# The first 18 microseconds of a state-space scan with a gated feed-forward: C's rows, the sums and half of g in another order

## The chip, the cores and the metric

The kernel runs on one core of a Trainium2 chip. A core has five engines that take their instructions in order, each from its own queue: TensorE (PE, with its weight loads shown as PEld), VectorE (DVE), ScalarE (ACT), GpSimd (POOL) and SyncE (SP), which here only issues DMAs. They meet at semaphores. The metric is the device time of one execution in microseconds; a run's figure is given with the median of several. All times below are of the profiled execution, counted from its start, unless said otherwise.

## The reference

Inputs are x (4 sequences, 8 heads, 768 steps, 32 channels), a (a decay for each step), B and C (16 state components). Weights are w_in (256 x 2048) and w_out (2048 x 256), which arrive in 8-byte floats.

```python
# per sequence and head, in chunks of 32 steps
cum = np.cumsum(log(clip(a, 1e-6, 1)))
L = exp(cum[i] - cum[j]) * (i >= j)
y_intra = ((C @ B.T) * L) @ x
y_inter = (C @ state) * exp(cum)
y = y_intra + y_inter
state = exp(sum(la)) * state + sum_j B[j] x[j] * exp(cum[-1] - cum[j])
# then, with the heads' channels side by side (256), for 3072 rows
h = y @ w_in
out = (h * cos(h)) @ w_out
```

## The kernel before

The 768 steps are cut into six chunks of 128. Chunk 0, with which this document deals, is cut again into two units of 64 steps (k = 0 and 1) of all four sequences, so that the feed-forward can begin early. For a unit the kernel makes, in this order of need:

- **lam**, the decays between all pairs of steps: `share_a` spreads a's rows on DVE and POOL, `spread_a` (L372) multiplies them by a 0/1 matrix on PE into a bank called a_ps, `decays0` (L380) scans the bank on DVE. Unit 0 is spread in four products of 256 columns, (k, p, i) = (0,0,0) to (0,1,1), unit 1 in (1,0,0), (1,0,1) and the whole of (1,1), which is two records of 512 columns. A float32 product shows as two records on PE.
- **the turned C and B**: C's first 128 rows of each sequence come as four DMAs (`load_c`, L113) in groups of four rows. A copy into `c0` puts them in order of row (columns 0 to 2 of four on POOL at L358, column 3 on ACT at L918). `turn_c` (L403) transposes c0 by four products and gives back `take(k)`, two scaled copies on ACT into `cuts[k]`, and `of`, a plain copy. `turn_b` (L418) transposes B's rows of a unit and copies them on ACT.
- **g**, the products of C and B (`inner(k, t)`, L461, t = 0 and 1 for the heads' halves, 16 small products each); **m**, g weighted by lam (`weights(k, q)`, L472, DVE); **sc**, B weighted by lam's last column (`weigh0`, L391, POOL).
- **y** and the new state (`finish0(k)`, L514): for unit 1 first the old state's part (L527, 32 products), then `sums` (L480, called in finish0: sc with x, 32 products, the state's sum), then m with x (L537, 64 products). y is copied on ACT to `yT`, the sums to `state0` by `take`. For unit 1 the old state's part needs `rT`, C weighted by the reach (`reach0`, L424, a product and a DVE scan, and `weigh_c`, L433, with a plain copy of C on ACT and a product on POOL).

The feed-forward goes in steps n. Step n of chunk 0 takes unit n % 2 and 256 columns of w_in: `first(n)` (L662) makes hp in two halves e, four records each half, and can run a function between the halves; `wind_k`, `wind_w`, `gate` and `gated` make hp * cos(hp) on ACT and DVE; `second(n)` (L797) adds its product with w_out to the output. A piece of weights is fetched as pairs of 32-bit words (`fetch`, L226) and turned to float32 by `grade` (L244: ACT, POOL, ACT) and `join` (L266: two DVE operations and an addition on POOL, L283).

Three things set the order of the work. Each engine runs its instructions in the order of the text below L909, which is written out by hand. SP's queue is the order of the fetches and loads at L285 to L302: a, B of unit 0, w_in 0, x of unit 0, B of unit 1, w_in 1, x of unit 1, w_out 0 and on; ACT's queue holds the four loads of C. And PSUM's banks are lent out by turns: `pair` (L72) gives two banks at a time out of two such pairs (to the first two spread products, to each half of g, to y of unit 0 once and to y of unit 1 twice), `bank` with the tags "h" and "o" gives single banks out of two each. A product into a buffer that was lent before waits until the last reader of the earlier content is done.

From L1060 on `first_steps` runs steps 0 to 3 with unit 1's y between the halves of step 0:

```python
        for q in range(2):
            weights(1, q)
        states_of = []
        first(0, lambda: states_of.extend(finish0(1)))
```

Of the kernel before, what the change touches and what calls it, by code (L numbers as in the profile page):

```python
# [8 lines left out]
FP32 = mybir.dt.float32  # L9
# [16 lines left out]
def kernel(  # L26
# [236 lines left out]
        if later:  # L263
            return rest

    def join(which, i, between=None):  # L266


        parts = held.pop((which, i), ())
        for e, (high, bits, last) in enumerate(parts):  # L270
            V.tensor_scalar(out=bits, in0=bits, scalar1=3, scalar2=0x3FFFFFFF,
                            op0=ALU.logical_shift_left, op1=ALU.bitwise_and)
            if between:
                between()
            V.scalar_tensor_tensor(out=bits, in0=high, scalar=0xC0000000, in1=bits,
                                   op0=ALU.bitwise_and, op1=ALU.bitwise_or)
            dst = kept(which, i)
            if len(parts) > 1:
                dst = dst[:, :, e * P:(e + 1) * P]
            else:  # L280
                bits, last = (ap.rearrange("p (k f) -> p k f", k=dst.shape[1])
                              for ap in (bits, last))
            G.tensor_tensor(out=dst.bitcast(U32), in0=bits, in1=last, op=ALU.add)  # L283

    for b in range(NB):  # L285
        load_c(b, nc.scalar)
    for s in range(2):
        load_b(0, s)
    fetch("in", 0)
# [1 line left out]
        load_x(0, s)  # L291
    for s in range(2):
        load_b(1, s)
    fetch("in", 1)
    for s in range(2):
        load_x(1, s)
    fetch("out", 0)
    nc.sync.dma_start(
        out=a_in, in_=a.rearrange("(u b) h (c p) -> (b h c) u p", u=NU, p=P))
# [47 lines left out]
    whose_of(1)  # L347
    G.memset(along1[:, :, 0:1], 0.0)
    G.tensor_scalar(out=a0[:, 1], in0=a0[:, 1], **clip)
    for p in range(2):  # L350
        G.tensor_tensor(out=along1[:, 2 * p:2 * p + 2, 1:], in0=a0[:, 1:2].to_broadcast([P, 2, W]),
                        in1=those[:, p::2].unsqueeze(2).to_broadcast([P, 2, W]), op=ALU.mult)
    own = ms[2][:, 3 * NB * (W + 1):3 * NB * (W + 1) + P]
    G.tensor_copy(out=own.rearrange("p (h n) -> p h n", h=H),
                  in_=mine.unsqueeze(2).to_broadcast([P, H, N]))
    c0 = loads.tile([P, 2, 2, 4, 2, N], FP32, tag="blocks", name="c0").rearrange(
        "p a b c d n -> p (a b c d n)").rearrange("p (r h n) -> p r h n", r=4, h=H)
    G.tensor_copy(out=c0[:, 0:3].rearrange("p r h n -> p h r n"), in_=c4[:, :, 0:3])  # L358
    G.memset(lead, 0.0)
    G.memset(lead[:, :, 0:1], 1.0)  # L360
    slot = const.tile([P, 2], FP32, name="slot")
# [68 lines left out]
            out=reach1.rearrange(flat), data0=ps.rearrange(flat),  # L430
            data1=lead.rearrange(flat), initial=0.0, op0=ALU.mult, op1=ALU.add)

    def weigh_c(k, of):  # L433
        c = scan.tile([P, NB, W], FP32, tag="rT", name="c1")
        of(k, c)
        rTs[k] = t = scan.tile([P, NB, W], FP32, tag="rT", name="rT")
        G.tensor_tensor(out=t, in0=c, in1=reach1[:, :, 1:], op=ALU.mult)

# [72 lines left out]
                                       scalar=reach[k // 2, s][:, p, i:i + 1],  # L511
                                       in1=after[k][:, s, p], op0=ALU.mult, op1=ALU.add)

    def finish0(k):  # L514

        m, xk = m_of[k], xrs[k]
        y = [pair("y") for _ in range(2)] if k else [pair("y")]
        at_ = [[(y[t][:, s, p * W:(p + 1) * W] if k else
                 y[0][:, s, t * P + p * W:t * P + (p + 1) * W]) for p in range(2)]
               for t in range(2) for s in range(2)]  # L520
        if k:
            old = states0.pop(k)
            for p in range(2):
                for s in range(2):
                    for q in range(4):
                        r, c0 = slice(32 * q, 32 * q + 32), W * (q % 2)
                        PE.matmul(at_[2 * (q // 2) + s][p][c0:c0 + W], lhsT=old[r, s, p],  # L527
                                  rhs=rTs[k][r, 2 * p + s], start=(p == 0), stop=False,
                                  tile_position=(32 * q, c0), skip_group_check=True)
        sums(k, [y[0][:, s, 3 * P:] for s in range(2)], lambda q, s: slice(32 * q, 32 * q + 32),  # L530
             start=(k == 0))
        for p in range(2):
            for t in range(2):
                for s in range(2):
                    ss = slice(s * W, (s + 1) * W)
                    for q in range(4):
                        PE.matmul(at_[2 * t + s][p][32 * q:32 * q + 32],  # L537
                                  lhsT=xk[ss, p, 4 * t + q], rhs=m[ss, p, 4 * t + q],
                                  start=False, stop=True,
                                  tile_position=(s * W, 32 * q), skip_group_check=True)  # L540
        if k % 2 == 0:
            yT[k // 2] = two.tile([P, 2, 2, 2 * P], FP32, tag="yT", name="yT")
        t_ = yT[k // 2][:, k % 2]
        if k:
            for t in range(2):
                ACT.copy(out=t_[:, t].rearrange("p (s i) -> p s i", s=2), in_=y[t][:, :, 0:P])
        else:
            ACT.copy(out=t_.rearrange("p t (s i) -> p s t i", s=2),
                     in_=y[0][:, :, 0:2 * P].rearrange("p s (t i) -> p s t i", t=2))
        states0[k + 1] = new = states.tile([P, 2, 2, 2 * D], FP32, tag="state0", bufs=2,  # L550
                                           name="state0")

        def take():
            for t in range(2):
                ts = slice(t * D, (t + 1) * D)
                ACT.activation(new[:, :, :, ts], y[0][:, :, 3 * P:].rearrange(
                    "p s (q d) -> p s q d", q=2)[:, :, :, ts], AF.Copy, scale=slot[:, t:t + 1])

        def add():
            dec = scan.tile([P, 2, 2, 2 * D], FP32, tag="whole", bufs=1, name="whole")  # L560
            r4 = reachs[k].rearrange("p (q s) i -> p s q i", s=2)
            for s in range(2):
                G.tensor_tensor(out=dec[:, s], in0=old[:, s],
                                in1=r4[:, s, :, W:].to_broadcast([P, 2, 2 * D]), op=ALU.mult)
            if k < 3:
                G.tensor_tensor(out=new, in0=new, in1=dec, op=ALU.add)
                return
            whole = states.tile([P, 2, 2, 2 * D], FP32, tag="state1", bufs=1, name="state1")
            for s, to_ in ((1, new), (0, whole)):
                G.tensor_tensor(out=to_[:, s], in0=new[:, s], in1=dec[:, s], op=ALU.add)  # L570
            after[3] = whole

            def exchange():
                for qs, rs in turns_of[1]:
                    nc.sync.dma_start(out=whole[rs, 1], in_=new[32 * qs.start:32 * qs.stop, 1])
            return exchange
        return take, add

    def reaches(c, b):

# [333 lines left out]
    for p, i in ((0, 0), (0, 1), (1, 0)):  # L914
        decays0(0, p, i, 2)
    tp_b = bank([P, 4, P], "tp", "o")
    turn_b(0, tp_b)()
    ACT.copy(out=c0[:, 3:4].rearrange("p r h n -> p h r n"), in_=c4[:, :, 3:4])  # L918
    spread_a(0, 1, 1, 2, "h")
    decays0(0, 1, 1, 2)  # L920
    take_c, of_c = turn_c()
    spread_a(1, 0, 0, 2, "h")
    take_c(0)
    decays0(1, 0, 0, 2)
    weigh0(0)
    grade("in", 0)
    for t in range(2):
        inner(0, t)
    spread_a(1, 0, 1, 2, "h")
    spread_a(1, 1, tag="h")  # L930
    for q in range(2):
        weights(0, q)
    take_c(1)
    join("in", 0)
    decays0(1, 0, 1, 2)
    decays0(1, 1)
    take_s0, _ = finish0(0)
    take_b = turn_b(1, tp_b)
    scan_reach = reach0(1)
    scan_reach()  # L940
    take_b()
    take_s0()
    for t in range(2):
        inner(1, t)
    weigh0(1)
    weigh_c(1, of_c)

    la = const.tile([RB, NU, P], FP32, name="la")
    cut = const.tile([RB, NU, P], FP32, name="cut")
# [110 lines left out]
    def first_steps():  # L1060

        grade("in", 1)
        for q in range(2):
            weights(1, q)
        states_of = []
        first(0, lambda: states_of.extend(finish0(1)))
        take_s1, add_s1 = states_of
        join("in", 1)
        rests = [grade("out", 0, later=True)]
        wind_k(0)  # L1070
        take_s1()
        rests.pop()()
        wind_w(0)
        first(1)
        join("out", 0)
        wind_k(1)
        gate(0)
        wind_w(1)
        gate(1)
        gated(0)  # L1080
        gated(1)
        first(2, tag=None)
        rests = [grade("in", 2, later=True)]
        wind_k(2)
        rests.pop()()
        clip_cut()
        wind_w(2)
        rests = [grade("out", 1, later=True)]
        join("in", 2)
        first(3, tag=None)  # L1090
        gate(2)
        wind_k(3)
        rests.pop()()
        rests = [grade("in", 3, later=True)]
        gated(2)
        join("out", 1)
        second(0)
        wind_w(3)
        gate(3)
        rests.pop()()  # L1100
        rests = [grade("out", 2, later=True)]
        join("in", 3)
        gated(3)
        second(1)
        clip_all()
        return add_s1, rests
# [166 lines left out]
```

## Time and profile before

| | |
|---|---|
| median of 3 runs | 364.44 us (363.73 to 365.11) |
| the profiled execution's own time | 364.44 us |
| its span from first to last instruction | 362.7 us |
| mean granted TensorE clock | 0.998 |
| PE busy, 0 to 6.2 us / 6.2 to 17.67 / 17.67 to 40 | 5.43 / 10.59 / 22.29 us |
| ACT busy in the same stretches | 1.49 / 6.09 / 18.74 us |
| DVE | 5.00 / 8.99 / 19.73 us |
| POOL | 3.91 / 5.76 / 15.98 us |
| DMA engines, mean busy share | 0.60 / 1.00 / 0.67 |

The first stretch lasts until TensorE leaves the first three spread products, the second until it begins the second half of step 0, and the third is the first part of the feed-forward. Busy time on PE counts pipelined products from start to modelled end, so it is nearly full even where the array works on small products. Idle time ahead of an instruction is put down to whatever semaphore came last. A DMA's issue and its landing are different marks: the issue is an instruction on SP or ACT, the landing is the last of 16 semaphore steps.

### The profile page before, as it was taken

The numbers are of one execution on the slowest core, as the hardware profiler recorded it, in microseconds if no ns is written. First come the engines' busy times: TensorE is split into PE (matmuls) and PEld (weight loads), VectorE is DVE, ScalarE is ACT, GpSimd is POOL, SyncE is SP. The second block draws the span as 40 slices with busy tenths as digits, with TensorE's granted clock in tenths as the row PEclk, the third lists the DMA queues.
The fourth block names the chain that finished last, engine by engine and source line by source line (L and its number), as shares of the span: only waits on it lengthen the run. The fifth ranks groups of instructions, "written<-read, shape, count | busy, mean of one in ns | idle before, by whom it ended". The sixth has DMA issues, their size and how long they took to land.

```text
span 362.7 us, 10240 instructions
## 1 busy us (share of the span) xinstructions
PE 357.0 (98%) x4070; PEld 326.0 (90%) x4070; DVE 276.0 (76%) x504; ACT 184.0 (51%) x352; POOL 239.7 (66%) x387
## 2 busy tenths in 40 slices
PE   8999999999999999999999999999999999999995
PEld 4788888889999999999989999999999999999995
DVE  7779998488876987878766877875776776688864
ACT  3597656544454346534536533545553544444552
POOL 5567767699666677674786666686666465475572
PEclk9999999999999999999999999999999999999999
DMA  7984997666583429113228202110001001001001
GB/s 138 246 284 141 189 196 122 85 125 98 134 129 58 99 51 135 14 34 76 53 53 119 23 3 75 28 33 11 0 2 31 0 3 33 0 3 29 3 17 44
DMA packets 96624, 26.43 MB, mean 73 GB/s; under 512 B 86624, under 2 KB 92480, under 8 KB 96576
## 3 DMA queue, kind: packets, MB, share of 16 engines
q1 hardware_dynamic: 95328, 25.38, 34.9%
q8 instruction: 32, 0.52, 0.6%
q10 hardware_dynamic: 1248, 0.39, 0.5%
q14 instruction: 16, 0.13, 0.1%
HBM read 22.36 MB, written 3.34 MB: 71 GB/s over the span
## 4 chain that ended last, share of the span: by engine, by line
PE 96%; DMA 2%; DVE 1%; issue 0%; ACT 0%; POOL 0%; DVEq 0%
PE o L848 35%; PE hp L672 33%; PE o L808 8%; PE m L772 7%; PE hp L772 5%; DMA bc<-in_C_dram 2%; PE y L641 2%; PE g L615 1%; PE y L489 1%; PE y L629 1%; PE g L468 1%; PE y L537 1%; PE y L527 1%; PE o L900 0%; PE tp L451 0%
## 5 line engine op out<-in xcount | busy, mean ns | idle before, releaser
L672 PE MATMUL hp<-yT,w_in 128*128 128x256 f32 x544 | 129.6, 382 | 0.1
L672 PEld LDWEIGHTS hp<-yT,w_in 128*128 128x128 f32 x544 | 99.0, 190 | 13.8 <-issue 1.4
L724 POOL TENSOR_TENSOR gd<-gT 128x256 f32<-128x256 f32 x79 | 58.1, 735 | 76.9 <-DVE gT L699 61.8
L694 ACT ACTIVATE w<-w,quarter 128x512 f32<-128x512 f32 x96 | 69.4, 723 | 65.8 <-DVE w L685 65.7
L685 DVE SCALAR_TENSOR_TENSOR w<-hp,k 128x512 f32<-128x512 f32 x96 | 65.8, 686 | 45.4 <-ACT k L679 45.2
L679 ACT ACTIVATE k<-hp 128x512 int32<-128x512 f32 x96 | 57.2, 596 | 68.6 <-PE hp L672 60.3
L699 DVE TENSOR_TENSOR gT<-hp,w 128x512 f32<-128x512 f32 x96 | 65.6, 683 | 12.2 <-ACT w L694 8.3
L848 PE MATMUL o<-words,gd 128*128 128x128 f32 x474 | 66.0, 275 | 0.0
L848 PEld LDWEIGHTS o<-words,gd 128*128 128x128 f32 x474 | 59.4, 192 | 0.0
L848 PE MATMUL o<-w_out,gT 128*128 128x128 f32 x316 | 50.4, 278 | 0.0
L848 PEld LDWEIGHTS o<-w_out,gT 128*128 128x128 f32 x316 | 45.4, 191 | 3.1
L726 POOL TENSOR_TENSOR gd<-gT,gd 128x128 f32<-128x128 f32 x79 | 39.6, 501 | 6.2
L727 POOL TENSOR_TENSOR gd<-gT,gd 128x128 f32<-128x128 f32 x79 | 39.0, 493 | 6.2
L848 PE MATMUL o<-w_out,gd 128*128 128x128 f32 x158 | 30.6, 276 | 0.0
L848 PE MATMUL o<-words,gT 128*128 128x128 f32 x158 | 30.6, 275 | 0.0
L808 PE MATMUL o<-w_out,gT 128*128 128x256 f32 x128 | 30.0, 380 | 0.0
L387 DVE TENSOR_TENSOR_SCAN lam<-arow,unit 128x512 f32<-128x512 f32 x20 | 29.9, 1496 | 0.1
L808 PEld LDWEIGHTS o<-w_out,gT 128*128 128x128 f32 x128 | 24.2, 190 | 3.6 <-POOL w_out L283 0.4
L848 PEld LDWEIGHTS o<-words,gT 128*128 128x128 f32 x158 | 24.0, 192 | 0.0
L848 PEld LDWEIGHTS o<-w_out,gd 128*128 128x128 f32 x158 | 24.0, 192 | 0.0
L772 PE MATMUL m<-m,words 128*128 128x128 f32 x168 | 23.4, 276 | 0.0
L772 PE MATMUL hp<-yT,w_in 128*128 128x128 f32 x112 | 21.7, 275 | 0.0
(130 smaller groups left out, 463.6 us busy)
## 6 DMA issues: line engine op xcount, KB each, us to landing
words<-in_moe_w_in_dram SPq DMA_DIRECT2D x8, 512.0 KB
words<-in_moe_w_out_dram SPq DMA_DIRECT2D x8, 512.0 KB
xr<-in_x_dram SPq DMA_DIRECT2D x24, 128.0 KB
arow<-a_cut SPq DMA_DIRECT2D x10, 256.0 KB
arow<-a_cut SPq DMA_DIRECT2D x10, 252.0 KB
out_dram<-sum SPq DMA_DIRECT2D x18, 128.0 KB
bc<-in_B_dram SPq DMA_DIRECT2D x24, 64.0 KB
blocks<-in_B_dram SPq DMA_DIRECT2D x16, 32.0 KB
```

The lines of the kernel that those rows point to most:

```text
L387: V.tensor_tensor_scan(out=lams[k][:, p, hs].rearrange(flat), data0=rows_.rearrange(flat), data1=unit0[:, hs].rearrange(flat), initial=0.0 ...
L672: PE.matmul(to_[:, e], lhsT=w_in[:, k, fs], rhs=y[:, k], start=(k == 0), stop=(k == KT - 1), skip_group_check=True)
L679: ACT.activation(k, hp[n], AF.Copy, bias=0.25, scale=INV_2PI)
L685: V.scalar_tensor_tensor(out=w, in0=hp[n], scalar=INV_2PI, in1=k, op0=ALU.mult, op1=ALU.subtract)
L694: ACT.activation(cos, cos, AF.Sin, bias=quarter, scale=TWO_PI)
L699: V.tensor_tensor(out=gT[n], in0=hp.pop(n), in1=cos, op=ALU.mult)
L724: G.tensor_tensor(out=d[:, 0:2], in0=g[:, 1:2].to_broadcast([P, 2, P]), in1=g[:, 3::-3], op=ALU.subtract)
L726: G.tensor_tensor(out=d[:, 2], in0=g[:, 0], in1=d[:, 0], op=ALU.subtract)
L727: G.tensor_tensor(out=d[:, 3], in0=g[:, 2], in1=d[:, 2], op=ALU.subtract)
L772: PE.matmul(dst[q], lhsT=w[q], rhs=y_[q], start=(q in (6, 1, 7)), stop=True, skip_group_check=True)
L808: PE.matmul(o[c, u][:, t], lhsT=g[:, 2 * e + t], rhs=w_out[:, 2 * j + e], start=(j == e == t == 0), stop=(j == NJ - 1 and e == 1), skip_gr ...
L848: PE.matmul(at[q], lhsT=a_[q], rhs=w[q], start=(j == 0 and q in starts), stop=(j == NJ - 1), skip_group_check=True)
```

## The change

C's fourth load goes from ACT's queue to SP's, where it stands behind a and ahead of B. On SP the loads of x of unit 1 go ahead of w_in 1. C's rows are copied in one operation on POOL, ahead of the products for `along1`; ACT's share of that copy is gone. C is transposed and its scaled copies for unit 0 are made ahead of B's transposes, and with them ahead of the spread (0,1,1). The spread (1,1) goes behind `sums` of unit 0, inside `finish0`, and for both units `sums` stands first, ahead of all of y. The copy of y of unit 0 goes behind B's copy of unit 1 on ACT. `join` of w_in 0 adds in two halves of 128 columns. The plain copy of C (`copy_c`) is made just behind `take_c(1)`, `weigh0(1)` goes ahead of the reach's scan. g of unit 1 is split: its first half stays ahead of step 0, its second half, with its weights on DVE, goes between the halves of step 0, ahead of `finish0(1)`.

```diff
@@ -263,7 +263,7 @@
         if later:
             return rest
 
-    def join(which, i, between=None):
+    def join(which, i, between=None, halves=False):
 
 
         parts = held.pop((which, i), ())
@@ -280,10 +280,15 @@
             else:
                 bits, last = (ap.rearrange("p (k f) -> p k f", k=dst.shape[1])
                               for ap in (bits, last))
+            if halves:
+                for f in (slice(0, P), slice(P, 2 * P)):
+                    G.tensor_tensor(out=dst[:, :, f].bitcast(U32), in0=bits[:, :, f],
+                                    in1=last[:, :, f], op=ALU.add)
+                return
             G.tensor_tensor(out=dst.bitcast(U32), in0=bits, in1=last, op=ALU.add)
 
-    for b in range(NB):
-        load_c(b, nc.scalar)
+    for i in range(NB):
+        load_c(i, nc.scalar if i < NB - 1 else nc.sync)
     for s in range(2):
         load_b(0, s)
     fetch("in", 0)
@@ -291,9 +296,9 @@
         load_x(0, s)
     for s in range(2):
         load_b(1, s)
-    fetch("in", 1)
     for s in range(2):
         load_x(1, s)
+    fetch("in", 1)
     fetch("out", 0)
     nc.sync.dma_start(
         out=a_in, in_=a.rearrange("(u b) h (c p) -> (b h c) u p", u=NU, p=P))
@@ -347,15 +352,15 @@
     whose_of(1)
     G.memset(along1[:, :, 0:1], 0.0)
     G.tensor_scalar(out=a0[:, 1], in0=a0[:, 1], **clip)
+    c0 = loads.tile([P, 2, 2, 4, 2, N], FP32, tag="blocks", name="c0").rearrange(
+        "p a b c d n -> p (a b c d n)").rearrange("p (r h n) -> p r h n", r=4, h=H)
+    G.tensor_copy(out=c0.rearrange("p r h n -> p h r n"), in_=c4)
     for p in range(2):
         G.tensor_tensor(out=along1[:, 2 * p:2 * p + 2, 1:], in0=a0[:, 1:2].to_broadcast([P, 2, W]),
                         in1=those[:, p::2].unsqueeze(2).to_broadcast([P, 2, W]), op=ALU.mult)
     own = ms[2][:, 3 * NB * (W + 1):3 * NB * (W + 1) + P]
     G.tensor_copy(out=own.rearrange("p (h n) -> p h n", h=H),
                   in_=mine.unsqueeze(2).to_broadcast([P, H, N]))
-    c0 = loads.tile([P, 2, 2, 4, 2, N], FP32, tag="blocks", name="c0").rearrange(
-        "p a b c d n -> p (a b c d n)").rearrange("p (r h n) -> p r h n", r=4, h=H)
-    G.tensor_copy(out=c0[:, 0:3].rearrange("p r h n -> p h r n"), in_=c4[:, :, 0:3])
     G.memset(lead, 0.0)
     G.memset(lead[:, :, 0:1], 1.0)
     slot = const.tile([P, 2], FP32, name="slot")
@@ -430,9 +435,12 @@
             out=reach1.rearrange(flat), data0=ps.rearrange(flat),
             data1=lead.rearrange(flat), initial=0.0, op0=ALU.mult, op1=ALU.add)
 
-    def weigh_c(k, of):
+    def copy_c(of):
         c = scan.tile([P, NB, W], FP32, tag="rT", name="c1")
-        of(k, c)
+        of(1, c)
+        return c
+
+    def weigh_c(k, c):
         rTs[k] = t = scan.tile([P, NB, W], FP32, tag="rT", name="rT")
         G.tensor_tensor(out=t, in0=c, in1=reach1[:, :, 1:], op=ALU.mult)
 
@@ -511,13 +519,19 @@
                                        scalar=reach[k // 2, s][:, p, i:i + 1],
                                        in1=after[k][:, s, p], op0=ALU.mult, op1=ALU.add)
 
-    def finish0(k):
+    def finish0(k, between=None):
 
         m, xk = m_of[k], xrs[k]
         y = [pair("y") for _ in range(2)] if k else [pair("y")]
         at_ = [[(y[t][:, s, p * W:(p + 1) * W] if k else
                  y[0][:, s, t * P + p * W:t * P + (p + 1) * W]) for p in range(2)]
                for t in range(2) for s in range(2)]
+        at = [y[0][:, s, 3 * P:] for s in range(2)]
+        strip = lambda q, s: slice(32 * q, 32 * q + 32)
+        if k < 2:
+            sums(k, at, strip, start=True)
+        if between:
+            between()
         if k:
             old = states0.pop(k)
             for p in range(2):
@@ -527,8 +541,8 @@
                         PE.matmul(at_[2 * (q // 2) + s][p][c0:c0 + W], lhsT=old[r, s, p],
                                   rhs=rTs[k][r, 2 * p + s], start=(p == 0), stop=False,
                                   tile_position=(32 * q, c0), skip_group_check=True)
-        sums(k, [y[0][:, s, 3 * P:] for s in range(2)], lambda q, s: slice(32 * q, 32 * q + 32),
-             start=(k == 0))
+        if k > 1:
+            sums(k, at, strip)
         for p in range(2):
             for t in range(2):
                 for s in range(2):
@@ -544,7 +558,8 @@
         if k:
             for t in range(2):
                 ACT.copy(out=t_[:, t].rearrange("p (s i) -> p s i", s=2), in_=y[t][:, :, 0:P])
-        else:
+
+        def take_y():
             ACT.copy(out=t_.rearrange("p t (s i) -> p s t i", s=2),
                      in_=y[0][:, :, 0:2 * P].rearrange("p s (t i) -> p s t i", t=2))
         states0[k + 1] = new = states.tile([P, 2, 2, 2 * D], FP32, tag="state0", bufs=2,
@@ -574,7 +589,7 @@
                 for qs, rs in turns_of[1]:
                     nc.sync.dma_start(out=whole[rs, 1], in_=new[32 * qs.start:32 * qs.stop, 1])
             return exchange
-        return take, add
+        return (take, add) if k else (take_y, take, add)
 
     def reaches(c, b):
 
@@ -914,36 +929,34 @@
     for p, i in ((0, 0), (0, 1), (1, 0)):
         decays0(0, p, i, 2)
     tp_b = bank([P, 4, P], "tp", "o")
+    take_c, of_c = turn_c()
+    take_c(0)
     turn_b(0, tp_b)()
-    ACT.copy(out=c0[:, 3:4].rearrange("p r h n -> p h r n"), in_=c4[:, :, 3:4])
     spread_a(0, 1, 1, 2, "h")
     decays0(0, 1, 1, 2)
-    take_c, of_c = turn_c()
     spread_a(1, 0, 0, 2, "h")
-    take_c(0)
     decays0(1, 0, 0, 2)
     weigh0(0)
     grade("in", 0)
     for t in range(2):
         inner(0, t)
     spread_a(1, 0, 1, 2, "h")
-    spread_a(1, 1, tag="h")
     for q in range(2):
         weights(0, q)
     take_c(1)
-    join("in", 0)
+    c1 = copy_c(of_c)
+    join("in", 0, halves=True)
     decays0(1, 0, 1, 2)
+    yT0, take_s0, _ = finish0(0, lambda: spread_a(1, 1, tag="h"))
     decays0(1, 1)
-    take_s0, _ = finish0(0)
-    take_b = turn_b(1, tp_b)
+    weigh0(1)
+    turn_b(1, tp_b)()
     scan_reach = reach0(1)
     scan_reach()
-    take_b()
+    weigh_c(1, c1)
+    yT0()
     take_s0()
-    for t in range(2):
-        inner(1, t)
-    weigh0(1)
-    weigh_c(1, of_c)
+    inner(1, 0)
 
     la = const.tile([RB, NU, P], FP32, name="la")
     cut = const.tile([RB, NU, P], FP32, name="cut")
@@ -1060,10 +1073,15 @@
     def first_steps():
 
         grade("in", 1)
-        for q in range(2):
-            weights(1, q)
+        weights(1, 0)
         states_of = []
-        first(0, lambda: states_of.extend(finish0(1)))
+
+        def unit1():
+            inner(1, 1)
+            weights(1, 1)
+            states_of.extend(finish0(1))
+
+        first(0, unit1)
         take_s1, add_s1 = states_of
         join("in", 1)
         rests = [grade("out", 0, later=True)]
```

## The prediction

> **What bounds the kernel now.** The page's line of engines comes first: TensorE (PE) is busy 98% of a span of 362.7 us. Its chain of work that ended last is PE's to 96%. So time can only be won where the chain is not PE work. The chain in order of time shows where that is (start, length, what):
>
> ```profile
> 2.99 3.89 DMA bc<-in_C_dram
> ...
> 6.93 0.52 POOL c L358
> ...
> 7.49 0.67 PE tp L407 x4
> ...
> 8.19 0.85 ACT cT L411 x2
> ...
> 9.08 0.71 PE g L468 x30
> ...
> 17.02 0.72 PE y L537 x39
> 17.74 6.24 PE hp L672 x28
> ```
>
> The fourth load of C, its copy on POOL, its turn on PE and the scaled copies on ACT lead to unit 0's products g. From 17.7 us on nearly every piece is PE's, back to back. So the whole change is worth what it moves one instruction: the first hp matmul of the second half of step 0, which starts at 17.67. I call this moment E. Everything ahead of E is filled with waits; everything behind it follows E one for one, unless a later wait takes over.
>
> The timeline of PE (start, span, instructions; in brackets idle time before and its cause) gives the order that the change alters:
>
> ```profile
> 9.08 0.73 PE L468 MATMUL g<-cT,turned 32*64 32x128 f32 x32 [0.50 <-ACT cT L411]
> 9.73 1.56 PE L376 MATMUL a_ps<-m 128*128 128x256 f32 x4
> 11.22 0.45 PE L489 MATMUL y<-xr,sc 64*32 64x64 f32 x32
> 11.49 0.90 PE L537 MATMUL y<-m,xr 64*32 64x64 f32 x64
> 12.32 0.44 PE L421 MATMUL tp<-ident,bc 128*128 128x128 f32 x2
> 12.81 0.71 PE L427 MATMUL a_ps<-m 128*128 128x260 f32 x2
> 13.45 1.09 PE L468 MATMUL g<-cT,turned 32*64 32x128 f32 x32
> 14.47 1.13 PE L672 MATMUL hp<-yT,w_in 128*128 128x256 f32 x4
> 15.53 1.11 PE L527 MATMUL y<-rT,state 32*64 32x64 f32 x32
> ```
>
> The reader sees g of unit 0, three spread products' records (L376), sums (L489), y (L537), then unit 1's preparation, half of hp 0 (L672), and the start of y of unit 1 (L527).
>
> **C's rows.** The four loads of C on ACT's queue are issued at 0.74, 1.20, 1.69 and 2.99 and land at 2.97, 3.37, 4.56 and 6.88 (the trace's landing marks). The fourth issue stands from 2.17 to 2.99 for the landing of the first. Moved to SP it takes the place of B's first load, issued at 1.19 and landed at 4.63. B's load is 1024 packets of 64 bytes, the C load 256 of 256, so it should be no later: I take all of C at 4.6, 2.3 us earlier. It pushes SP's later issues by one issue, some 0.46 us (a C issue on ACT).
>
> On the skill: a rule speaks against this part. "DMA: Bandwidth & Descriptors", Issuing engines are not separate DMA queues, says that all issuing engines end on the same 16 DMA engines, so another issuer saves only the issuing sequencer's time, usually small. By that rule alone the landing moves by about one issue, to 6.4, C is copied by 7.1, and E comes later, not earlier, since what is put behind C slips. The rows above show more than issue time: a wait of 0.82 us for a landing, and a place ahead of 2048-byte packets. I go by the rows.
>
> The copy was 0.51 us for 384 columns on POOL, and 0.30 for 128 on ACT. As one copy on POOL it is 0.51 x 512/384 = 0.68, from 4.65 to 5.33. It is hidden: PE runs the first three spread products until 6.2. What POOL does behind it (L351 1.23, L354 0.28, memsets 0.42) ends at 7.3 in place of 7.9, still ahead of weigh0's need (DVE's scans of unit 0, 8.4).
>
> **Turn of C ahead of B.** PE reaches the transposes of C where it reached B's, at 6.21. Four take 0.67 and some 0.1 for slower first records (B's two started 0.24 apart): ready at 7.0 in place of 8.16. ACT's two scaled copies (0.85) end at 7.87. B's copy, which ran free at 6.80, now comes behind them: 0.37, from 7.76 to 8.14. So g of unit 0 starts at 8.17, not 9.08, a gain of 0.91. The price is paid by lam: the spread (0,1,1) starts at 7.1, not 6.60; its scan starts at 7.72, not 7.24, and the next, which waited for PE at 8.62, at 8.33. So the weights of unit 0 (L477, 1.29) run from 8.94 to 10.24, in place of 11.10, and join's DVE part ends at 11.3 in place of 12.16. All this is a gain of about 0.87.
>
> **Sums ahead of the last spread, and that ahead of y.** This is where I expect most of it to be lost. PE would be ready for sums at 8.17 + 0.66 (g) + 0.64 (one spread of two records) = 9.47. But sums read x of unit 0, and its second load landed at 9.88. Before, the spread (1,1) ran in that time (10.27 to 11.13), and sums at 11.22 had x for long. Now PE stands in line for x, and the spread of 0.86 comes after. From the start of sums, s, to the first y: 0.27 sums, 0.17 to change shape, 0.43 and 0.52 for the two records of 512: 1.40 us (before: 0.27).
>
> When does x land? Between 4.5 and 8.2 us the DMA engines are full, and the fourth C load's 256 packets of 18 ns (0.29 us of 16 engines) are among them. These move to 2.5 to 3.1 us, where the engines were 0.4 to 0.8 busy. Against that stands the 0.46 us by which SP issues later; from 3.9 to 4.5 the engines were but half busy, so this can be made up. Bounds: 9.47 or earlier (then PE decides) and 9.88 + 0.5 = 10.38. I take 9.88 - 0.29 = 9.59, the nearer to the packets' own rows, so s = 9.63.
>
> **From sums to E.** Each step is the distance between the same rows before: first y s + 1.40; to reach0's matmul 1.16 (12.49 + 0.16 less 11.49; its buffer is free at 11.9, earlier than needed); to g of unit 1's first half 0.64; to hp 0's first half 0.60 (16 products at 0.40, 0.20 change); to g's second half 1.06; its result 0.68; weights(1,1) on DVE with its two hand-overs 0.72; PE's answer 0.04. Sum 6.30: y of unit 1 may open its second buffer at s + 6.30 = 15.93. It has to wait for that: the pool has two pairs of banks, and the second pair of y is the one that weights(1,1) reads. Before, the same release came at 15.66, PE going at 15.70. So the half of g put behind hp 0 makes this release 0.23 later, though all ahead of it is earlier. What pays for it: sums of unit 1 (0.27 and a change of shape 0.15) now run inside that wait, and the gap of 0.25 that PE shows at 16.05 within y, with no cause in the profile, falls at the same count of instructions into the wait too. Left behind the release are 28 products of L527 at 0.45, a change 0.15, 64 products 0.83: 1.43, against 1.97 before. E = 15.93 + 1.43 = 17.36, against 17.67: **-0.31 us**.
>
> Hidden, worth nothing: w_in 0 in halves (POOL 11.4 to 12.7, hp 0 starts at 13.4, cover 0.7); c1's copy (0.40) moved from 13.69 to 10.5 on ACT; weigh0(1) ahead of the reach scan (POOL idle). yT of unit 0 behind B's copy on ACT: 12.6 to 13.2, with PE asking at 13.4, cover 0.2. x of unit 1 takes w_in 1's place and w_in 1 the last place: landing 14.59 in place of 12.94. ACT's grade of it starts at 14.6, not 13.95, and ends at 15.9; behind it on ACT waits yT of unit 1 (17.3), cover 1.4; w_in 1 is complete near 18.7, and first read at 20. If it lands over 1.4 us later still, hp 1 is late by the rest.
>
> Against the profiled execution (364.44 us, which is also the median) this gives 364.1.
>
> **Rivals.** (a) x of unit 0 decides to the bad: each us that it lands past 9.95 makes E later than before (s + 7.73 = 17.67 at s = 9.94), at one for one. At 10.38 it is +0.5, with the gap at 16.05 still there +0.75: 364.9 to 365.2. For it: 9.88 before is already next to the point, and SP issues later. Against: C's packets leave the full stretch. (b) It is given back: PE waits at 27.25 for w_in 2 from POOL (27.21). If that chain is bound by ACT's and POOL's own work, PE arrives earlier and waits: no change, 364.4. For: ACT is 84% busy from 17.7 to 40 (18.74 of 22.33). Against: that ACT work starts with yT of unit 1, so it moves along. (c) The gain at g is kept whole, if x is there and y's second buffer does not hold PE: 0.9 less, 363.5. Against: the same buffer held PE at 15.70. (d) The edit doesn't do what it says: SP's C load or what follows waits for an earlier landing, as ACT's did from 2.17 to 2.99. SP then starts B and x some 1.8 us later, s = 11.7, E = 19.4: 366.2. Eight loads are under way here before one is waited for, which speaks against it.
>
> **Chances.** Forecast 0.50, (a) 0.24, (b) 0.18, (c) 0.05, (d) 0.03. The shown runs spread from 363.73 to 365.11, 0.7 to each side, more than any of (a) to (c) apart. The range takes the forecast's bounds (s at 9.47: -0.47) and (a)'s, with half that spread below: 363.2 to 365.2. Half a per cent, about what a measurement of this kernel can tell from no change, is 1.8 us: only (d) reaches it, and nothing found reaches it on the fast side, so within 0.5% 0.94, slower 0.04, faster 0.02.
>
> **What would show it.** C's copy on POOL before 5.5; transposes L407 at 6.2; g of unit 0 near 8.2; a wait of PE ahead of L489 near 9.5 whose end is a DMA of x; y of unit 0 ending near 12.0; a wait near 15.5 to 15.9 ahead of L527 ended by DVE's L477; no gap within L527; E near 17.4. Wrong would be: no wait for x (then E is earlier, to 17.2), transposes held by POOL's copy, or PE waits between 20 and 40 us that grow by what E gained.

## The result, and the profile after

The changed kernel takes 364.99 us (median of 22 runs, 364.14 to 366.6) against 364.18 for the kernel before in the same series (363.46 to 365.11): a ratio of 1.0026, 95% interval 1.0015 to 1.0037. The forecast was 0.3 us faster; it is 0.8 us slower, inside the stated range of 363.2 to 365.2 but on the other side of the kernel before. The profiled execution of the kernel after took 366.32 us (span 364.5), one of its slower ones.

PE's timeline of the kernel after in the first 18 us, columns as before the change:

```profile
5.98 0.60 PE L412 MATMUL tp<-ident,c 128*128 128x128 f32 x4
...
7.78 0.73 PE L476 MATMUL g<-cT,turned 32*64 32x128 f32 x32
...
9.30 0.32 PE L497 MATMUL y<-xr,sc 64*32 64x64 f32 x8 [0.17 <-DVE m L485]
10.01 0.43 PE L497 MATMUL y<-xr,sc 64*32 64x64 f32 x24 [0.39 <-DMA xr<-in_x_dram]
10.37 1.13 PE L381 MATMUL a_ps<-m 128*128 128x512 f32 x2
11.42 0.86 PE L551 MATMUL y<-m,xr 64*32 64x64 f32 x64
...
15.74 0.33 PE L541 MATMUL y<-rT,state 32*64 32x64 f32 x4
16.24 0.68 PE L541 MATMUL y<-rT,state 32*64 32x64 f32 x28 [0.17 <-DVE m L485]
16.85 0.86 PE L551 MATMUL y<-m,xr 64*32 64x64 f32 x64
17.64 1.13 PE L687 MATMUL hp<-yT,w_in 128*128 128x256 f32 x4
```

g of unit 0 starts at 7.78, 1.3 us early; then sums wait for x (10.01), y for the product of g with lam (16.24), and E is 17.64: as in the profile before, to 0.03. So in this execution the head itself lost nothing. The loss is behind it. The page's chain is no longer PE's to 96%:

```profile
PE 89%; SPq 4%; DMA 3%; POOL 1%; DVE 1%; issue 1%; ACT 1%; DVEq 0%; ACTq 0%; POOLq 0%
```

and in order of time (start, length, what) it names a transfer:

```profile
9.95 6.66 DMA words<-in_moe_w_in_dram
...
16.63 0.69 ACT mag L258
...
17.40 0.62 POOL mag L259
...
19.35 1.27 POOL w_in L288
20.62 0.59 POOL mag L259
...
27.06 1.26 POOL w_in L288
...
28.36 3.72 PE hp L687 x16
```

w_in 1 is under way for 6.66 us, and POOL adds it up until 20.62. From there the chain goes over POOL, DVE and ACT with the next pieces until w_in 2 is added at 28.3. PE, which began its fifth step at 27.27 before, begins it at 28.36. The same additions on POOL and PE's fifth step in the kernel before:

```profile
17.21 1.27 POOL L283 TENSOR_TENSOR w_in<-mag,last 128x512 uint32<-128x512 uint32 x1 [1.34 <-DVE mag L275]
...
25.92 1.28 POOL L283 TENSOR_TENSOR w_in<-mag,last 128x512 uint32<-128x512 uint32 x1
...
27.27 3.06 PE L672 MATMUL hp<-yT,w_in 128*128 128x256 f32 x13
```

There w_in 1 was added 2.1 us earlier, at 18.48, and w_in 2 at 27.20, 0.07 us ahead of PE.

### The profile page after: what moved, and what is told of

Read it like the earlier page. It is cut to its first block, busy times and chain, and to the rows that moved or that the text cites. A ratio compares the mean times of both kernels' runs of the same rounds, so it can differ in the third digit from the quotient of the medians.

```text
span 364.5 us, 10240 instructions
## 1 busy us (share of the span) xinstructions
PE 357.7 (98%) x4070; PEld 326.1 (89%) x4070; DVE 276.7 (76%) x504; ACT 183.7 (50%) x351; POOL 238.3 (65%) x388
## 4 chain that ended last, share of the span: by engine, by line
PE 89%; SPq 4%; DMA 3%; POOL 1%; DVE 1%; issue 1%; ACT 1%; DVEq 0%; ACTq 0%; POOLq 0%
PE o L863 34%; PE hp L687 30%; PE m L787 7%; PE o L823 6%; PE hp L787 5%; DMA words<-in_moe_w_in_dram 2%; PE y L656 2%; PE g L630 1%; SPq L108 1%; PE y L644 1%; PE y L497 1%; SPq L151 1%; SPq L123 1%; DMA blocks<-in_C_dram 1%; POOL w_in L288 1%
## 5 line engine op out<-in xcount | busy, mean ns | idle before, releaser
L741 POOL TENSOR_TENSOR gd<-gT,gd 128x128 f32<-128x128 f32 x79 | 40.3, 511 | 6.2
L742 POOL TENSOR_TENSOR gd<-gT,gd 128x128 f32<-128x128 f32 x79 | 37.4, 473 | 6.2
L392 DVE TENSOR_TENSOR_SCAN lam<-arow,unit 128x512 f32<-128x512 f32 x20 | 30.7, 1536 | 2.7 <-DMA arow<-a_cut 2.7
```

The costliest lines, as they stand in the source:

```text
L392: V.tensor_tensor_scan(out=lams[k][:, p, hs].rearrange(flat), data0=rows_.rearrange(flat), data1=unit0[:, hs].rearrange(flat), initial=0.0 ...
L741: G.tensor_tensor(out=d[:, 2], in0=g[:, 0], in1=d[:, 0], op=ALU.subtract)
L742: G.tensor_tensor(out=d[:, 3], in0=g[:, 2], in1=d[:, 2], op=ALU.subtract)
```

## A table of seventeen profiles

The experiments are read through this table. E is the start of hp 0's second half. "w_in 1" gives the sixteenth, last landing mark of its DMA, and ahead of it the fifteenth where the two are compared below. "d" is the time from E to the fifth step. "At 84" is how far PE's work slips against the kernel before between 80 and 90 us. All in us, all from the traces. (The trace of the kernel after holds only fifteen marks of x of unit 0; 9.96 is the last of these, and PE goes on at 10.01.)

| kernel | time | x of unit 0 | w_in 1 | E | d | at 84 |
|---|---|---|---|---|---|---|
| before | 364.44 | 9.88 | 12.94 | 17.67 | 9.60 | - |
| before_again | 363.97 | 9.42 | 12.45 | 17.12 | 9.60 | 0 |
| before_third | 364.53 | 9.63 | 12.77 | 17.75 | 9.60 | 0 |
| after | 366.32 | 9.96 | 14.94 / 16.61 | 17.64 | 10.72 | 0.91 |
| after_again | 365.04 | 9.55 | 14.13 / 15.27 | 17.23 | 9.78 | 1.02 |
| after_third | 365.40 | 9.75 | 14.89 / 16.39 | 17.43 | 10.71 | 0 |
| after_fourth | 365.89 | 9.68 | 14.77 / 16.65 | 17.36 | 11.05 | 0 |
| before_x1_first | 364.12 | 9.58 | 13.97 | 17.16 | 9.60 | 0 |
| w_in1_first | 364.25 | 9.57 | 12.60 | 17.61 | 9.60 | 0 |
| spread_first | 366.49 | 9.90 | 15.59 / 17.55 | 18.14 | 11.14 | 0 |
| both_back | 364.59 | 9.65 | 12.63 | 17.72 | 9.60 | 0 |
| c_early | 363.73 | 9.60 | 12.79 | 16.95 | 9.60 | 0 |
| c_early_x1_first | 365.18 | 9.80 | 14.56 | 17.89 | 9.60 | 0 |
| after_b_late | 364.52 | 9.39 | 15.56 / 15.79 | 17.31 | 10.21 | 0 |
| c_early_b_late | 364.24 | 9.81 | 12.83 | 17.34 | 9.60 | 0 |
| both_mended | 363.84 | 9.35 | 13.33 | 17.18 | 9.60 | 0 |
| both_mended_g_whole | 364.31 | 9.77 | 12.94 | 17.82 | 9.60 | 0 |

Two things can be read off. d is 9.60 wherever w_in 1 landed by 14.6, and longer in each row where it landed past 15.2. And E moves by 0.6 between executions of the kernel before itself. A sum closes the account: the time less E, d and the slip at 84 is 337.2 to 337.3 us in the three profiles of the kernel before and 337.0 to 337.5 in the four of the kernel after, so these columns hold the loss to a few tenths.

## The experiments

Theory: w_in 1, moved behind x of unit 1, comes too late, and POOL's queue hands the delay on. Rivals: sums ahead of the spread make unit 0 wait for x; something later in the run.

**The swap on SP and the order of sums, each undone alone, both, and the swap alone.**

w_in1_first, against the kernel after:

```diff
+    fetch("in", 1)
     for s in range(2):
         load_x(1, s)
-    fetch("in", 1)
```

spread_first, against the kernel after (in `finish0`):

```diff
+        if between:
+            between()
         if k < 2:
             sums(k, at, strip, start=True)
-        if between:
-            between()
```

both_back is the two together; before_x1_first is the kernel before with the swap alone.

> The changed kernel with one edit taken back: on SP w_in 1 goes ahead of x of unit 1 again. Theory: w_in 1 landing at 16.6 us (12.9 before) makes POOL add it at 19.4 to 20.6, and every weight piece behind it on POOL and DVE is 1.1 us late, so that PE waits at the fifth step. Then here w_in 1 lands by 14, ACT grades it at 14, PE no longer waits for its addition, and the time is 0.7 to 1.2 us below the changed kernel: 363.8 to 364.4 against 364.2 of before. Rival: the new order on PE, ACT and POOL costs the time and w_in 1's place is covered, as the prediction had it; then this run stays at 364.8 to 365.2.

> The changed kernel with the spread (1,1) ahead of sums of unit 0 again, so that PE works while x of unit 0 is on its way (it landed at 9.96, and PE began the second half of sums at 10.0). Theory: y of unit 0 and step 0 come 0.5 to 1.0 us earlier, but w_in 1's addition ends at 20.6 all the same, so the time stays that of the changed kernel: 364.7 to 365.1. Rival (PE's order decides the time): 0.5 to 1.0 below it, 364.0 to 364.4.

> The changed kernel with both taken back: w_in 1 ahead of x of unit 1, the spread (1,1) ahead of sums of unit 0. Theory: with w_in 1 early, what PE gains ahead of step 0 now reaches the end, unless x of unit 1, now the later one, holds the sums of unit 1: 363.2 to 364.0. Rival: as the changed kernel less what the spread alone gains, 364.0 to 364.4.

> The kernel before with that one edit of the change alone: x of unit 1 ahead of w_in 1 on SP. Theory: w_in 1 lands at 14.6 at best and up to 2 us later; its grade starts on ACT when it lands and not at 13.95; slower than before by 0.3 to 1.2 us, 364.5 to 365.4. Rival (its place is covered): within 0.2 us of before.

Measured, medians against 364.01 for the kernel before: w_in1_first 364.31 (ratio 1.0008, 0.9999 to 1.0016), spread_first 365.08 (1.0027, 1.0017 to 1.0036), both_back 364.48 (1.0022, 1.0008 to 1.0036), before_x1_first 364.17 (1.0003, 0.9994 to 1.0013). Putting w_in 1 back alone takes most of the loss away, as the theory had it; putting the order of sums back alone takes none. both_back missed its theory and its rival: three of its twelve runs lie at 365.9 to 366.5, the other nine at 364.06 to 364.78, and its one profile is of the faster kind and doesn't show why. So w_in 1 in its old place is not by itself a sure cure in every version. That the swap alone cost nothing on top of the kernel before was a miss: there w_in 1 was issued at 9.37 and landed at 13.97, in time; in the kernel after it was issued at 9.67 to 9.95, behind one load more. So it isn't the swap by itself that cost, but the swap together with the rest of the change. In w_in1_first PE runs on from E without a wait:

```profile
17.61 6.31 PE L687 MATMUL hp<-yT,w_in 128*128 128x256 f32 x28
23.76 3.62 PE L823 MATMUL o<-w_out,gT 128*128 128x256 f32 x16
27.21 3.05 PE L687 MATMUL hp<-yT,w_in 128*128 128x256 f32 x13
```

**C's part alone, without and with the swap.** c_early is the kernel before with the fourth load of C on SP, the one copy on POOL and C's first turn ahead of B's; c_early_x1_first adds the swap.

```diff
-    for b in range(NB):
-        load_c(b, nc.scalar)
+    for i in range(NB):
+        load_c(i, nc.scalar if i < NB - 1 else nc.sync)
...
+    take_c, of_c = turn_c()
+    take_c(0)
     turn_b(0, tp_b)()
```

> The kernel before with the change's first part alone: C's fourth load on SP, C copied in one operation on POOL, turned and scaled ahead of B. All else as before: the spread (1,1) ahead of sums, g of unit 1 whole, w_in 1 ahead of x of unit 1. Theory (the early C is a gain, and what follows it in the change gives it back): g of unit 0 starts near 8.1, the second half of step 0 at 16.8 to 17.3 in place of 17.7, w_in 1 lands at 13: 363.3 to 363.8. Rival (PE is held just ahead of that half by x of unit 1 or by its own instructions, whatever C does): 363.9 to 364.2.

> The same, and x of unit 1 ahead of w_in 1 on SP. Theory: the instruction block of 16 KB that a DMA engine carries near 12.7 us falls ahead of w_in 1's last packets, w_in 1 lands near 16, and its addition holds PE two steps later: 0.4 to 1.1 above the run with the early C alone. Rival (w_in 1's place is covered): within 0.2 of it, or below it where x of unit 1 held PE.

Measured against 364.43: c_early 364.09 (0.9994, 0.9985 to 1.0003), c_early_x1_first 365.19 (1.0025, 1.0014 to 1.0035). c_early's E, 16.95, is where its theory had it, but its time is not clear of no change. With C early the swap costs 0.3%, as much as the whole change. In its one profile w_in 1 was in time (14.56) and d 9.60; there E is 0.9 later than in c_early, behind a gap of PE from 15.06 to 16.53 (in c_early 14.39 to 15.26). So most of the 1.45 us by which this execution is behind c_early's came with a later E, and none with a late w_in 1. Whether the swap brings the longer gap about, and how often each way comes, one profile doesn't show.

**That gap.** Eight profiles show PE standing still at 14 to 16.5 us with no cause in the trace. In the third profile of the kernel before, the last of 27 products of L527 starts 0.92 us before the next; 0.70 of that PE is idle:

```profile
14.94 0.74 PE L527 MATMUL y<-rT,state 32*64 32x64 f32 x27
16.39 0.33 PE L527 MATMUL y<-rT,state 32*64 32x64 f32 x5 [0.70 <-issue]
```

The page lists a queue "q8 instruction" with 32 packets of 16 KB, 0.52 MB; the 8140 instructions of PE and PEld are 254 for each. The first such packet inside the run starts at 11.6 to 13.9 us and takes 0.9 to 2.2 us on one DMA engine. If PE waits for it, the gap belongs to a count of instructions, not to a line. more_products puts 64 more instructions of PE (16 small products of the identity, into a part of g's bank that is not read) ahead of g of unit 0 in both_back.

> The changed kernel with both edits taken back (as the run of that kind before), plus 16 products of 64 x 32 by 32 on the identity, ahead of g of unit 0 where PE is idle, into an unused part of g's bank: 64 more instructions on PE, under 0.3 us. Theory: PE's gap of 0.93 us within sums of unit 1, at 15.14 to 16.07 in that run, is a wait for its next block of instructions, and the block of 16 KB seen on a DMA queue at 13.2 is that block; it is asked for at a place in the program. Then the block here starts 1 to 2 us earlier, PE's gap there is gone, and the second half of step 0 starts up to 0.9 earlier, unless x of unit 1 takes the gap's place. Rival (the block comes at its own time, the gap is the data's): the block stays near 13.2 and the gap at 15 to 16.

```profile
13.89 0.65 PE L482 MATMUL g<-cT,turned 32*64 32x128 f32 x12
15.14 0.43 PE L482 MATMUL g<-cT,turned 32*64 32x128 f32 x4 [0.59 <-issue]
...
16.99 0.81 PE L557 MATMUL y<-m,xr 64*32 64x64 f32 x59
21.98 0.43 PE L557 MATMUL y<-m,xr 64*32 64x64 f32 x5 [4.18 <-issue]
```

372.1 us (1.0221, 1.0199 to 1.0243): far slower, where the theory had expected the gap to go away and E to come up to 0.9 us earlier. The packet did start earlier (12.07, not 13.19). But the gap moved with it, from within sums (both_back) to within g, and stayed at the same count: behind the 219th or 220th matmul record in all eight profiles, with y, sums or g standing there. It ends 1.26 to 1.9 us after the packet does. A second gap of 4.4 us stands 127 matmuls, 254 instructions, further on, and the next packet ends at 20.4. So PE waits for its instructions here: the gap follows the count of instructions and the packet, not the line. Why the next packet started as late as 19.4 is not shown.

**The second loss.** Two of four profiles of the kernel after lose another microsecond at 84 us. DVE's and then PE's timeline of after_again:

```profile
82.19 1.23 DVE L392 TENSOR_TENSOR_SCAN lam<-arow,unit 128x512 f32<-128x512 f32 x1 [2.83 <-DMA arow<-a_cut]
83.33 0.67 DVE L714 TENSOR_TENSOR gT<-hp,w 128x512 f32<-128x512 f32 x1
```

```profile
84.05 1.99 PE L687 MATMUL hp<-yT,w_in 128*128 128x256 f32 x8 [0.66 <-DVE gT L714]
```

The scan waits for cut rows of A; gT stands behind it on DVE; PE waits for gT. The rows are late because SP is: it issues them at 79.9 (81.4 in the other execution), not 77.7, having lost 0.7, 0.9 and 1.0 us in three issues (51, 56 and 67 us) that took 3.0, 4.4 and 1.8 us in place of 2.3, 3.5 and 0.8. Why these took longer, and why in two of four executions, isn't shown. after_b_late and c_early_b_late move four loads that are needed last to behind them:

```diff
-        for k in (4, 5):
-            for s in range(2):
-                load_b(k, s)
...
                 load_arow(n - NF + 8)
+            if n == NF - 3:
+                for k in (4, 5):
+                    for s in range(2):
+                        load_b(k, s)
```

> The kernel after, with SP's four loads of B for units 4 and 5 issued behind the cut rows of A for the same units (two of them, four DMAs) instead of some twenty issues ahead of them; nothing is left out. In both profiled executions of the kernel after, PE waits at 84 to 85 us for a gT that stands behind a scan on VectorE, and that scan for the cut rows of A, which SP issues 2.4 to 2.7 us later against PE than in the kernel before (79.9 and 80.6 against 77.1 us and PE 0.25 us early). Theory (SP's lag is a real second cost of the kernel after, about 0.9 us in most executions): the cut rows are issued some 3 us earlier, the wait of PE at 84 us is gone, the median is 0.5 to 0.9 us lower than that of the kernel after, ratio to before 1.0000 to 1.0012. Rival (the lag belongs to the two profiled executions): the same PE stretch, median as before the move, ratio 1.0020 to 1.0030. Rival (B of units 4 and 5 or the rows of blocks now come late): a new wait of PE for bc or blocks at 82 to 92 us, ratio above 1.003.

> C's part of the change alone (fourth load of C on SP, one copy on POOL, its first turn ahead of B's) with the same move of the four loads of B; nothing is left out. C's part alone gave 364.09 us, ratio 0.9994, and its profiled execution had no wait of PE at 84 us. Theory (SP's lag costs only where the scan waits for the cut rows): nothing to win here, ratio 0.9985 to 1.0000. Rival (SP's queue costs something in most executions of every version): 0.3 to 0.9 us lower, ratio 0.997 to 0.9985.

Measured against 364.38: after_b_late 364.52 (1.0005, 0.9994 to 1.0015), c_early_b_late 364.24 (0.9997, 0.9988 to 1.0006). The scan in after_b_late starts at 79.77 without a wait. So the lag of SP is a cost of the kernel after; on top of C's part alone the same move gains nothing, as the theory had it.

**Both mended, and further profiles.** both_mended is after with both moves; both_mended_g_whole also puts the second half of g of unit 1, and its weights, back ahead of hp 0.

> The kernel after with w_in 1 back ahead of x of unit 1 on SP, and SP's four loads of B for units 4 and 5 behind the cut rows of A; nothing is left out. Theory (the two costs are the whole): 9.60 us from the second half of hp 0 to its fifth step, no wait of PE at 84 us, ratio to before 0.9985 to 1.0003. Rival (a third cost is left in the rest of the change): ratio 1.0005 to 1.0015, as with w_in 1 alone put back (1.0008).

> As both_mended, with both halves of g of unit 1 and of its weights ahead of hp 0 again; nothing is left out. Theory (the second product of g with lam, which ends at 15.8 to 16.2 us behind the half of hp 0, sets the start in the kernel after, and an instruction block of PE sets it in the other order): the second product ends near 15, PE waits up to 1.5 us near its 449th instruction instead, and the start is within 0.3 us of both_mended's; ratio within 0.001 of it. Rival (the split is what costs): the start 0.5 us earlier, ratio 0.0015 lower.

> The kernel before once more, for a second profile. Theory (the first instruction block that is fetched while the kernel runs, and the late sixteenth of the transfers it shares an engine with, move the start by some tenths from execution to execution): the second half of hp 0 starts between 16.9 and 17.7 us, with the gap of PE inside the turned rows or the sums of unit 1 again, 0.2 to 1.5 us long. Rival (the start is the same each time): 17.67 within 0.05.

> The kernel before, a third profile: theory (its start moves with the landing of x of unit 0, 9.4 us, and with the first instruction block) 16.9 to 17.7 us for the second half of hp 0; rival (17.12 was the odd one) 17.6 to 17.7.

> The changed kernel once more, for a second execution. Theory: x of unit 0 lands near 9.9 and ends PE's wait ahead of sums, w_in 1's sixteenth mark comes 1 us or more behind its fifteenth, its addition on POOL ends past 20 and PE waits for it at the third step. Rival (the first execution was an odd one): w_in 1 lands by 15 and no wait is seen.

> The kernel after once more, for a third profile. Theory (SP's lag is there in most executions of it): PE waits 0.4 to 0.8 us for gT near 84 us, and the fourth step starts 0.2 us early to 1.1 us late against the kernel before, by where w_in 1's sixteenth lands (14.1 to 16.6 us). Rival (the lag is chance): no wait near 84 us.

> The kernel after, a fourth profile: theory, from the second half of hp 0 to its fifth step 9.60 us plus what w_in 1's last mark is past 15.1 us; start of the second half 17.2 to 17.6; at 84 us a wait of PE of about 1 us or none.

Measured against 364.14: both_mended 364.39 (1.0005, 0.9996 to 1.0014), both_mended_g_whole 364.31 (1.0002, 0.9993 to 1.0012). Neither differs from the kernel before by what can be measured. By the ratios the two moves don't add: each alone brings 1.0026 to 1.0008 or 1.0005, and both leave 1.0005, the lower end of the rival's range. But with some 0.001 to each side of every ratio, two separate costs of about 0.5 us each fit as well. An overlap is possible, since in w_in1_first SP too was 1.3 us ahead of the kernel before at 54 us and the scan did not wait. How a median run divides between the two is not settled; nor is a third cost below 0.1% excluded. both_mended_g_whole is within 0.001 of it, as expected, but its E came 0.64 later than both_mended's, not within 0.3, and without the gap that was expected. after_third and after_fourth show no wait at 84 us: the lag comes in some executions, as the rival of after_third had it. In both_mended E is set by x of unit 1, now behind w_in 1 and the instruction packet:

```profile
15.01 0.84 PE L497 MATMUL y<-xr,sc 64*32 64x64 f32 x32 [0.18 <-DMA xr<-in_x_dram]
15.77 0.69 PE L541 MATMUL y<-rT,state 32*64 32x64 f32 x32
```

No version was clearly faster than the kernel before. c_early comes closest.

## Why the prediction was wrong

- **C's rows: right.** The last load landed at 4.37 (forecast 4.6), the copy ran 4.52 to 5.14 (4.65 to 5.33), g began at 7.78 (8.17 forecast, 9.08 before). The Trainium skill, "DMA: Bandwidth & Descriptors", Issuing engines are not separate DMA queues, by which the estimate was 6.4, was the worse guide here: the load had stood behind a wait for a landing, which the rule leaves out. It was issued at 1.18, not 2.99, and was under way 3.19 us, not 3.89.
- **Sums, spread, y: the mechanism right, the gain at its break-even.** PE waited for x of unit 0 as forecast, but x landed no earlier: 9.55 to 9.96 in four profiles, 9.42 to 9.88 in three of before; the 0.29 us expected from C's packets did not show. From x's landing to E it is 7.68 in all four profiles (forecast 7.77), with y's second buffer released by DVE at 15.77 to 16.19 (15.93). E is 17.23 to 17.64, mean 17.42 (17.36).
- **The 0.31 us: a matter of the reference.** The kernel before has E at 17.67, 17.12 and 17.75, mean 17.51. From g of unit 0 to E it is 8.33 to 8.34 us plus the instruction packet's gap in all three; the gap was 0.25, 0.43 and 0.92, and g began at 9.08, 8.36 and 8.49, as C's last load landed at 6.88, 6.15 and 6.17. So the execution from which I reckoned had the latest C and the shortest gap, and I took both as fixed. Against the mean the change gains 0.1. That the gap would fall into the wait ahead of y was right: none of the four profiles of the kernel after shows it. (The four records of L376 at 9.73 are two spread products, not three as I read them; no term rests on it.)
- **The step that failed** is "x of unit 1 takes w_in 1's place and w_in 1 the last place: landing 14.59 in place of 12.94", "cover 1.4". Its landing was sized well for fifteen of sixteen marks (14.13 to 14.94). The sixteenth came 1.1 to 1.9 us later. The trace doesn't name the engines, but the marks tell the same story in all profiles: up to the instruction packet (12.74 to 13.91 in the profiled execution) the last mark of a load mostly follows at once, and among the next transfers it comes late, at the most by 0.8 to 2.3 us from profile to profile, as if the engine that had carried the packet were that far behind. In the kernel before these were w_out 0 (16.01 / 17.20) and what came behind it, for which nobody waits. And the cover was not ACT's. From the landing it takes 4.00 us until POOL has added w_in 1 (16.61 to 20.62), then 7.68 until it has added w_in 2 (28.30); in the six profiles with a late w_in 1 both agree to 0.03. PE asks for w_in 2 at E + 9.60. So w_in 1 must land by E - 2.08, 15.15 to 15.56. Past that the excess is 1.05, 0.12, 1.04 and 1.37 in the four profiles; d shows 1.12, 0.18, 1.11 and 1.45. In after_b_late and spread_first it is 0.56 and 1.49 against 0.61 and 1.54.
- **Rivals.** (a) named the wait that came, at no loss. (b), a gain given back at w_in 2 on POOL, had the right place; but POOL's chain there was lengthened by w_in 1, not fixed: in the profiles of the table with w_in 1 in time POOL ended w_in 2 at E + 9.52 or 9.53, whatever E was, as the case against (b) had it. Nothing in the prediction looked at SP's queue past 18 us, where up to a microsecond more went.

## What to carry to other kernels

When two transfers change places, follow the one that goes back to the last engine that works on it, and count what that engine has to do next: the slack is the smallest along the chain, not that at the first reader. Profile the kernel before more than once when the gain in view is as large as the scatter of the moment on which it is reckoned. Where all sixteen marks are needed, look at the last but one as well: a gap between the two tells of an engine that was busy with something else.

## What the runs showed of the hardware

PE's instructions come as 16 KB packets, which the profile's page counts among the work of the 16 DMA engines, and the first one inside the run was not always hidden. It cost gaps of 0.25 to 1.5 us at a fixed count of instructions in eight profiles; the second cost 4.4 us in more_products. Among the transfers that landed behind the first, the last mark came late, at the most by 0.8 to 2.3 us from profile to profile. The Trainium skill, "Runtime: NRT & Kernel Launch", Instruction fetch mechanics, calls such a crossing mostly hidden. At the next two packets of the kernel before (20.6 and 24.6 us), amid long matmuls, PE ran on; in this head, where small products use up 254 instructions in 4.5 us (11.59 to 16.05) and the DMA engines are full, it did not. Which of the two matters no run tells apart.

A short wait was once followed by half the clock. In spread_first sums of unit 1 waited for x from 14.6 to 16.17, and the granted clock (the column behind POOL's) was 0.50 from 17.3 to 20.7:

```profile
13.00:17.30 4.30, 2.96 (x103) 2.08 (x111) 1.37 (x2) 0.22 (x1) 0.76 (x2) 1.00 1.00 318
17.30:20.70 3.40, 3.40 (x70) 2.78 (x60) 1.12 (x2) 2.78 (x6) 1.03 (x2) 0.50 1.02 375
20.70:24.00 3.30, 3.30 (x16) 2.90 (x16) 2.49 (x5) 2.51 (x7) 1.97 (x3) 0.99 1.01 373
```

The hp matmuls in it followed each other at 0.43 us in place of 0.216. In more_products, where PE stood for 4.4 us, the clock was at 0.5 from 19.2 to 26.1. The gap of c_early_x1_first (15.06 to 16.53), nearly as long as the wait in spread_first, was followed by no such stretch, so these runs give no length of wait from which it happens.
